# Five blocks of 464 and 448 tokens in place of six of 384 in the first mixing stage, and memory and normaliser loaded pair by pair

## The chip, the cores and the metric

The kernel runs on one core of a Trainium2 chip. The metric is the device time of one execution in microseconds (us), lower is better. The engines of the core are named as the profile names them: PE multiplies, PEld is its loading of weights, DVE, ACT and POOL work on vectors, and SP issues the DMAs.

## The reference

Three computations follow one another on 4 batches of 576 tokens, 2304 in all, with 8 heads of 64 in attention and 512 features after it:

```python
# attention, for each batch and head
a = softmax(causal(q @ k.T / sqrt(64)));  local = a @ v
q_p = where(q > 0, q, exp(q) - 1) + 1
mem = (q_p @ M_prev) / (q_p @ z_prev + 1e-6)
x = g * mem + (1 - g) * local            # g = sigmoid(beta), one number a head
# first mixing stage, 512 -> 2048 -> 512
h = x @ w_in;  y = (h - tanh(h)) @ w_out
# second mixing stage, 512 -> 1024 -> 512
h = y @ w_in2;  s = h * softmax(h)
out = (layernorm(s) * g_ln) @ w_out2
```

The weights of the two mixing stages are float64 in memory; the chip turns them into pairs of float32 numbers.

## The kernel before, in words

**Attention** goes through 16 pairs of heads. Its order is written out by hand in two tables, `PROLOGUE` and `PERIOD`, in which a word such as `load_q:3:-` is one step (name, pair relative to the present one, engine). SP issues every load in that order, so a DMA waits behind the ones before it. `load_batch` brings M_prev (tile `Md`, L110) and z_prev (tile `zb`, L115) for a whole batch of four pairs, at the start of a period. `x_mv` writes the finished pair into `xT` (L420), the transposed tokens.

**The first mixing stage** (`Moe1`) holds all tokens as `xT` and splits each value into a rounded high half `xh` (L573, ACT) and a low half (L575, POOL). The hidden features are cut into 8 slices of 256; for each slice it goes over the token blocks. `h_step` multiplies a block with the slice's `wi`: 2 x 12 multiplications (L589). ACT and DVE then form h - tanh(h) and its two halves (L600 to L603). `y_step` multiplies the result with `wo`: 4 x 6 multiplications (L616), into PSUM tiles `Y` that DVE adds into `yT` (L628 in slice 0, L630 later). Blocks stand one after the other in this order on PE: H of block n+1, Y of block n. A Y tile has two buffers for its first two feature groups and one for the others, so Y of block n+1 waits until DVE has taken Y of block n.

Beside that a `Weights` loader turns the float64 weights of later slices into two float32 halves, a chunk of 128 x 512 at a time: one step on ACT (L732), five on DVE (L734 to L748), a sum on POOL (L750; on DVE in the first blocks), for `w2o` a scaling on POOL (L753), then the high half on ACT (L757) and the low half on POOL (L759; on DVE in the first blocks). `pump` finishes the chunk in work and starts the next; it is called once after each block. Every engine keeps the order of the program.

While the last pairs of attention run, the H multiplications of blocks 0 and 1 of slice 0 stand between them on PE. Behind them come Y of blocks 0 and 1, H of block 2, then the usual order.

**The second mixing stage** (`Moe2`) goes through 18 tiles of 128 tokens: `h_mm` (L796), the maximum (`top`, L807), the norms (`norm`, L816 to L825), transposes (L835) and the output multiplication `o_mm` with the eight blocks of `w2o` (L865). The chunks of `w2o` that the loader has not turned by the end of the first stage are done between `norm(1)` and `top(2)`.

Of the kernel before, what the change touches and what calls it, by code (L numbers as in the profile page):

```python
# [15 lines left out]
P = 128  # L16
# [6 lines left out]
class Attention:  # L23
# [5 lines left out]
    def __init__(self, ap, sp, ps, tc, q, k, v, M_prev, z_prev, beta, xT, ident):  # L29
# [6 lines left out]
        self.read, self.done = 0, 0  # L36
# [380 lines left out]
    def x_mv(self, p):  # L417
        b, h0 = divmod(2 * p, self.H)
        xt, t0 = self.xT(b * self.S)
        self.nc.sync.dma_start(  # L420
            out=xt[:, h0 // 2, t0 : t0 + self.S].bitcast(F32), in_=self.x.pop(p)
        )
# [7 lines left out]
        f_z:0:- load_k:1:- f_red:0:- load_q:2:- k_hd:0:a:0 f_eps:0:- k_ld:0:a:0 s_mm:0:-:4  # L430
# [8 lines left out]
        s_exp:1:-:2 s_norm:0:-:2 s_norm:0:-:1 s_norm:0:-:3 q_lo:2:- load_q:3:- s_mm:2:-:4  # L439
# [8 lines left out]
        load_q:4:- s_mm:3:-:1 s_max:3:-:1 a_t:1:-:3 s_exp:2:-:3 s_max:3:-:2 q_t:3:- q_hi:3:a  # L448
# [19 lines left out]
        s_eps:0:- load_q:3:- q_hi:2:a s_exp:1:-:4 s_mm:1:-:0 s_max:1:-:2 a_pv:-1:-:1  # L468
# [6 lines left out]
    def run(self, filler):  # L475
# [11 lines left out]
        def emit(name, i, engine, part):  # L487
# [40 lines left out]
class Moe1:  # L528
# [5 lines left out]
    NB = 384  # L534

    def __init__(self, tc, w_in, w_out, wpool, tpool, loader):
# [7 lines left out]
        self.w, self.x, self.G = {}, {}, {}  # L544

# [34 lines left out]
    def h_step(self, s, n, H, per=0):  # L580

        nc, KD, KF, NB = self.nc, self.KD, self.KF, self.NB
# [15 lines left out]
        G = self.G[s, n] = self.tp.tile([P, 2, KF, NB], F32R, tag="G", name=f"G{s}_{n}", bufs=2)  # L598
        t = self.tp.tile([P, KF, NB], F32, tag="t", name=f"t{s}_{n}", bufs=1)
# [5 lines left out]
    def y_step(self, s, n, ps, yT):  # L605
        nc, KF, NB = self.nc, self.KF, self.NB
# [5 lines left out]
        for d in range(self.KD):  # L612
# [8 lines left out]
            y = yT[:, d, n * NB : (n + 1) * NB]  # L621
# [3 lines left out]
            if d == 3:  # L625
                y, src = yT[:, 2:4, n * NB : (n + 1) * NB], X[:, :, 0:NB]
# [250 lines left out]
def attention_moe_kernel(  # L877
# [7 lines left out]
    HT = NT // 2  # L885
# [7 lines left out]
    xl = ctx.enter_context(tc.tile_pool(name="xl", bufs=2))  # L893
# [229 lines left out]
```

## Time and profile before

| | us |
|---|---|
| median of 3 runs | 866.45 (865.75 to 867.38) |
| the profiled execution, its own time | 866.64 |
| its span in the trace | 864.8 |
| PE busy | 837.6 (97%) |
| DVE busy | 625.1 (72%) |
| ACT busy | 395.8 (46%) |
| POOL busy | 366.7 (42%) |

The span is what the profiler saw of the execution; 1.84 us of the execution's own time lie around it. A busy share is an average over the whole span, while the stages differ: attention fills the first 250 us, the first mixing stage goes to about 650 us, the second one to the end. A busy time of PE counts multiplications that overlap, so it says less than the start of one block and of the next.

### The profile page before, as it was taken

How to read it: one execution, taken by the hardware profiler on the slowest of the kernel's cores; microseconds unless marked ns; L12 is line 12 of the kernel's file. 1: busy time of each engine (PE TensorE's matmuls, PEld its weight loads, DVE VectorE, ACT ScalarE, POOL GpSimd, SP SyncE). 2: the span in 40 equal slices, each digit the busy share in tenths (PEclk: the TensorE clock that was granted, in tenths of full speed). 3: DMA queues.
4: the chain of work that ended last, by engine and by line, in shares of the span. 5: the costliest groups of instructions: out<-in, count | busy, mean ns of one | idle time of the engine just before them, and what ended most of it. 6: DMA issues, size and time to landing. Idle time of an engine off the chain costs nothing.

```text
span 864.8 us, 13784 instructions
## 1 busy us (share of the span) xinstructions
PE 837.6 (97%) x5016; PEld 752.5 (87%) x5016; DVE 625.1 (72%) x1215; ACT 395.8 (46%) x843; POOL 366.7 (42%) x453
## 2 busy tenths in 40 slices
PE   4999999999999899999999999999999999999998
PEld 3777777777789899999999999999998888888887
DVE  6888889988657877787777877775787655555553
ACT  5898888888744323323233232332322323323222
POOL 6968787887835333333333333430533111111110
PEclk9999999999999999999999999999999999999999
DMA  6896677565110211212112121220200000000001
GB/s 131 198 207 161 161 183 164 146 146 135 45 52 25 74 60 63 74 50 74 54 69 74 49 74 49 74 70 5 72 27 0 25 25 25 20 19 25 25 25 37
DMA packets 82372, 64.66 MB, mean 75 GB/s; under 512 B 63296, under 2 KB 63552, under 8 KB 82304
## 3 DMA queue, kind: packets, MB, share of 16 engines
q1 hardware_dynamic: 82304, 63.78, 27.3%
q8 instruction: 40, 0.66, 0.3%
q14 instruction: 28, 0.23, 0.1%
HBM read 40.90 MB, written 4.72 MB: 53 GB/s over the span
## 4 chain that ended last, share of the span: by engine, by line
PE 73%; DVE 1%; ACT 1%; issue 0%; ACTq 0%
PE Y L616 23%; PE H L589 23%; PE H L796 11%; PE T L835 2%; PE X L400 1%; PE T L381 1%; PE O9X L865 1%; PE O3X L865 1%; PE O13X L865 1%; PE O11X L865 1%; PE O7X L865 1%; PE O5X L865 1%; PE O1X L865 1%; PE O0X L865 1%; PE O15X L865 1%; PE O16S L865 1%
## 5 line engine op out<-in xcount | busy, mean ns | idle before, releaser
L616 PE MATMUL Y<-G,wo 128*128 128x384 f32 x1152 | 209.3, 337 | 3.0 <-DVE yT L628 2.2
L616 PEld LDWEIGHTS Y<-G,wo 128*128 128x128 f32 x1152 | 202.2, 189 | 3.6 <-ACT cva L732 2.5
L589 PE MATMUL H<-xh,wi 128*128 128x384 f32 x768 | 150.7, 337 | 0.0
L589 PEld LDWEIGHTS H<-xh,wi 128*128 128x128 f32 x768 | 134.8, 188 | 1.3 <-issue 0.8
L600 ACT ACTIVATE t<-H 128x768 f32<-128x768 f32 x48 | 39.1, 814 | 197.4 <-PE H L589 193.0
L750 POOL TENSOR_TENSOR cvw<-cvw,cva 128x512 f32<-128x512 f32 x44 | 56.8, 1291 | 164.6 <-DVE cva L748 121.9
L336 POOL TENSOR_SCALAR P<-P,sm,og 128x192 f32<-128x192 f32 (+4 forms) x160 | 105.8, 673 | 23.1 <-DVE sm L331 19.7
L319 ACT ACTIVATE P<-sc,mx 128x192 f32<-128x192 f32 (+4 forms) x160 | 88.8, 558 | 9.1 <-DVE mx L303 8.6
L796 PE MATMUL H<-w2i,Ys 128*128 128x512 f32 x384 | 90.0, 390 | 0.0
L796 PEld LDWEIGHTS H<-w2i,Ys 128*128 128x128 f32 x384 | 72.0, 188 | 15.0
L601 DVE TENSOR_TENSOR t<-H,t 128x768 f32<-128x768 f32 x48 | 45.9, 957 | 51.6 <-ACT t L600 51.6
L381 PEld LDWEIGHTS T<-ident,P 128*128 128x128 f32 x480 | 52.4, 141 | 35.0 <-DVE mx L303 11.1
L589 PE MATMUL H<-xT,wi 128*128 128x384 f32 x384 | 82.8, 337 | 0.0
L303 DVE CUSTOM_DVE_ANT_0 sc<-S,mask 128x64 f32<-128x64 f32 (+4 forms) x160 | 73.1, 486 | 11.5 <-PE S L289 9.1
L381 PE MATMUL T<-ident,P 128*128 128x128 f32 x480 | 73.2, 281 | 7.6 <-DVE mx L303 6.2
L630 DVE TENSOR_TENSOR yT<-Y,yT 128x384 f32<-128x384 f32 (+1 forms) x126 | 79.0, 683 | 0.0
L603 DVE TENSOR_TENSOR G<-t,G 128x768 fp32r<-128x768 f32 x48 | 46.3, 965 | 42.4 <-ACT G L602 42.4
L824 POOL TENSOR_TENSOR s<-s,nhalf 128x1 f32<-128x1 f32 x18 | 9.9, 551 | 153.3 <-DVE s L823 134.5
L602 ACT CAST G<-t 128x768 fp32r<-128x768 f32 x48 | 40.1, 835 | 63.6 <-DVE t L601 63.6
L589 PEld LDWEIGHTS H<-xT,wi 128*128 128x128 f32 x384 | 67.9, 188 | 0.1
L807 DVE TENSOR_REDUCE s<-H 128x1 f32<-128x1024 f32 x18 | 22.0, 1224 | 59.9 <-PE H L796 59.9
L289 PE MATMUL S<-KH,Qs 128*128 128x256 f32 (+3 forms) x192 | 56.2, 330 | 8.2 <-DVE Qs L182 5.3
(285 smaller groups left out, 1427.0 us busy)
## 6 DMA issues: line engine op xcount, KB each, us to landing
raw<-in_moe_w_in_dram SPq DMA_DIRECT2D x24, 512.0 KB, 3.7
raw<-in_moe_w_out_dram SPq DMA_DIRECT2D x24, 512.0 KB, 3.5
xT<-x SPq DMA_DIRECT2D x16, 288.0 KB, 2.4
out_dram<-ob SPq DMA_DIRECT2D x17, 256.0 KB, 2.0
KH<-KH SPq DMA_DIRECT2D x30, 144.0 KB, 2.8
KL<-KL SPq DMA_DIRECT2D x30, 144.0 KB, 2.7
q<-in_q_dram SPq DMA_DIRECT2D x16, 256.0 KB, 3.7
k<-in_k_dram SPq DMA_DIRECT2D x16, 256.0 KB, 3.6
```

Of the source, the lines that this page charges most:

```text
L289: nc.tensor.matmul(t[:, o + a : o + z], lh, K[:, a:z], start=(i == 0), stop=(i == 1), skip_group_check=True,)
L303: self.nc.vector.tensor_tensor_reduce(out=sc, in0=t[:, o : o + W], in1=self.mask[:, self.S - W :], scale=-0.125, scalar=3.0e38, op0=ALU.ad ...
L319: self.nc.scalar.activation(self._p(n, c), self.sc[c], AF.Exp, bias=self.mx[n][:, c : c + 1], scale=-1.0, accum_out=self.sm[n][:, c : c + 1],)
L336: self.nc.gpsimd.tensor_scalar(d, d, self.sm[n][:, c : c + 1], self.og[:, h : h + 1], ALU.mult, ALU.mult)
L381: nc.tensor.transpose(T[:, at : at + P], Pt[:, col : col + P], self.ident)
L589: nc.tensor.matmul(H[:, f], wi[:, wl, c, f * P : (f + 1) * P], self.x[n][xl][:, c], start=(i == 0), stop=(i == 3 * KD - 1),)
L603: nc.vector.tensor_tensor(G[:, 1], t, G[:, 0].bitcast(F32), ALU.subtract)
L616: nc.tensor.matmul(Y[d][:, 0:NB], wo[:, wl, f, d * P : (d + 1) * P], G[:, gl, f], start=(i == 0), stop=(i == 3 * KF - 1),)
L630: nc.vector.tensor_tensor(y, src, y, ALU.add)
L750: self.eng.tensor_tensor(w, w, a, ALU.add)
L796: nc.tensor.matmul(H[:, nh * 512 : (nh + 1) * 512], Y[:, yl, c, :], w2i[:, wl, c, nh * 512 : (nh + 1) * 512], start=(k == 0), stop=(k == 3 ...
L865: nc.tensor.matmul(O, L[:, ll, f, :], self.w2o[f][:, wl, a : a + w], start=(f == 0 and k == 0), stop=(f == KF - 1 and k == 2),)
```

## The change

The token blocks get a list of sizes, 464, 464, 464, 464 and 448, and tiles that were sized by 384 are sized by 464. The two tiles of `xT` hold 928 and 1376 tokens in place of 1152 each; a pair whose tokens cross that border takes two DMAs. `load_batch` becomes `load_mem`, which brings M_prev and z_prev of one pair, three DMAs, and stands in the two tables of attention behind `load_q`; there are three tiles `Md` of one pair each. `pump` is called twice after block 2 of each slice, so that six chunks go with five blocks. One block of `w2o` has a tile of its own in place of two, and three in place of two lie in the room of `xT`.

```diff
-        for i in range(2):
-            t = ap.tile([P, self.HP, P], F32, tag=f"Md{i}", name=f"Md{i}", bufs=1)
+        for i in range(3):
+            t = ap.tile([P, P], F32, tag=f"Md{i}", name=f"Md{i}", bufs=1)
...
-    def load_batch(self, b):
+    def load_mem(self, p):
         nc, D = self.nc, self.D
-        Md = self.Md[b % 2]
+        b, h0 = divmod(2 * p, self.H)
         for j in range(2):
-            nc.sync.dma_start(
-                out=Md[j * D : (j + 1) * D, :, j * D : (j + 1) * D],
-                in_=self.M[b].rearrange("(c j) d e -> j d c e", j=2)[j],
-            )
-        zb = self.zb[b] = self.ap.tile([P, self.HP, 2, D], F32, tag="zb", name=f"zb{b}")
+            a = slice(j * D, (j + 1) * D)
+            nc.sync.dma_start(out=self.Md[p % 3][a, a], in_=self.M[b, h0 + j])
+        z = self.zb[p] = self.ap.tile([P, 2, D], F32, tag="zb", name=f"zb{p}")
         nc.sync.dma_start(
-            out=zb.rearrange("p c j d -> p (c j d)"),
-            in_=self.z[b].rearrange("h d -> (h d)").partition_broadcast(P),
+            out=z.rearrange("p j d -> p (j d)"),
+            in_=self.z[b, h0 : h0 + 2].rearrange("h d -> (h d)").partition_broadcast(P),
         )
...
-        xt, t0 = self.xT(b * self.S)
-        self.nc.sync.dma_start(
-            out=xt[:, h0 // 2, t0 : t0 + self.S].bitcast(F32), in_=self.x.pop(p)
-        )
+        x = self.x.pop(p)
+        for out, a in self.xT(h0 // 2, b * self.S, self.S):
+            self.nc.sync.dma_start(out=out.bitcast(F32), in_=x[:, a : a + out.shape[1]])
...
-        s_eps:0:- load_q:3:- q_hi:2:a s_exp:1:-:4 s_mm:1:-:0 s_max:1:-:2 a_pv:-1:-:1
+        s_eps:0:- load_q:3:- load_mem:2:- q_hi:2:a s_exp:1:-:4 s_mm:1:-:0 s_max:1:-:2 a_pv:-1:-:1
...
-            if batch < self.B and before >= self.HP * (batch - 1):
-                self.load_batch(batch)
-                batch += 1
...
-    NB = 384
+    BLOCKS = (464, 464, 464, 464, 448)
+    NB = max(BLOCKS)
...
-            w2o_part(w2p.tile([P, 2, 2, DM], F32R, tag="w2o", name="w2o"), 2)
+            w2o_part(w2p.tile([P, 2, 1, DM], F32R, tag="w2o", name="w2o"), 1)
...
             else:
                 loader.pump()
+                if n == 2:
+                    loader.pump()
```

Three places show how the instructions move. On DVE, in slice 0 of the first mixing stage, before the change, from the end of the conversion behind block 2 (`cva` and `cvw` are the loader's tiles; `t_3` and `G_3` belong to block 3, `Y_2` to block 2, `wi` is the next slice's weight):

```order
L748 SCALAR_TENSOR_TENSOR cva<-raw,cva 128x512
L750 TENSOR_TENSOR cvw<-cvw,cva 128x512
L601 TENSOR_TENSOR t_3_3873<-H_3_3847,t_3_3873 128x768
L603 TENSOR_TENSOR G_3_3872<-t_3_3873,G_3_3872 128x768
L628 COPY yT<-Y_2_0_3878 128x384
L628 COPY yT<-Y_2_1_3879 128x384
L628 COPY yT<-Y_2_2_3880 128x2x384
L759 TENSOR_TENSOR wi_3723<-cvw,wi_3723 128x512
```

One conversion stands ahead of block 3's activation. The same place with the change:

```order
L739 TENSOR_SCALAR cva<-cvw 128x512
L741 SCALAR_TENSOR_TENSOR cva<-raw,cva 128x512
L743 TENSOR_TENSOR cvw<-cvw,cva 128x512
L752 TENSOR_TENSOR wi_3777<-cvw,wi_3777 128x512
L727 TENSOR_SCALAR cva<-cva 128x512
L730 TENSOR_SCALAR cva<-cva 128x512
L734 SCALAR_TENSOR_TENSOR cvw<-raw,cva 128x512
L739 TENSOR_SCALAR cva<-cvw 128x512
L741 SCALAR_TENSOR_TENSOR cva<-raw,cva 128x512
L743 TENSOR_TENSOR cvw<-cvw,cva 128x512
L593 TENSOR_TENSOR t_3_3940<-H_3_3914,t_3_3940 128x928
L595 TENSOR_TENSOR G_3_3939<-t_3_3940,G_3_3939 128x928
```

A whole second conversion, with the low half of the first ahead of it, now stands ahead of `t_3`, and Y of block 2 behind that as before.

On DVE, at the start of the second mixing stage (`s_1`, `e_1` belong to token tile 1, `s_2` and `H_2` to tile 2), before:

```order
L822 BN_AGGR s_1_7292<-s_1_7292 128x2
L823 TENSOR_SCALAR s_1_7292<-s_1_7292 128x1
L825 TENSOR_SCALAR e_1_7309<-e_1_7309,s_1_7292 128x1024
L807 TENSOR_REDUCE s_2_7350<-H_2_7325 128x1
L817 TENSOR_SCALAR s_2_7350<-s_2_7350 128x1
```

Here the last step of norm(1) is followed by the maximum of tile 2. With the change:

```order
L814 BN_STATS s_1_6837<-e_1_6854 128x6 x2
L815 BN_AGGR s_1_6837<-s_1_6837 128x2
L816 TENSOR_SCALAR s_1_6837<-s_1_6837 128x1
L818 TENSOR_SCALAR e_1_6854<-e_1_6854,s_1_6837 128x1024
L727 TENSOR_SCALAR cva<-cva 128x512
L730 TENSOR_SCALAR cva<-cva 128x512
L734 SCALAR_TENSOR_TENSOR cvw<-raw,cva 128x512
L739 TENSOR_SCALAR cva<-cvw 128x512
L741 SCALAR_TENSOR_TENSOR cva<-raw,cva 128x512
L800 TENSOR_REDUCE s_2_6907<-H_2_6882 128x1
```

The five DVE steps of one more `w2o` chunk stand between the two.

On SP, in the prologue of attention, before (`q`, `KH`, `KL`, `Qs` are the loads and moves of the scores):

```order
L127 DMA q_97<-in_q_dram 128x8x64
L131 DMA q_97<-in_q_dram 64x2x64
L184 DMA KH_1_283<-KH_1_283 64x576
L184 DMA Qs_115<-Qs_113 64x576
L184 DMA KL_1_284<-KL_1_284 64x576
```

The moves come right behind the load of q. With the change:

```order
L125 DMA q_97<-in_q_dram 128x8x64
L129 DMA q_97<-in_q_dram 64x2x64
L111 DMA Md_113<-in_M_prev_dram 64x64 x2
L113 DMA zb_336<-in_z_prev_dram 128x128
L182 DMA KH_1_289<-KH_1_289 64x576
L182 DMA Qs_117<-Qs_115 64x576
L182 DMA KL_1_290<-KL_1_290 64x576
```

Three DMAs for M_prev and z_prev stand ahead of the moves.

## Rows read from the trace of the kernel before

**Rows 1.** The table of stretches (`windows`): from and to in us from the start of the span and the length, then the busy time of PE, PEld, DVE, ACT and POOL with the instructions in brackets, the granted TensorE clock (1.00 is full), the busy share of the DMA engines, and GB/s. The stretches are the steady part of attention, the change from attention to the first mixing stage, the steady part of that stage, and the second mixing stage.

```profile
25.00:200.00 175.00, 168.35 (x1306) 132.00 (x1304) 154.96 (x426) 153.19 (x413) 140.66 (x211) 1.00 0.71 169
...
251.00:292.00 41.00, 38.02 (x209) 37.44 (x209) 30.56 (x39) 16.22 (x30) 19.96 (x18) 0.96 0.09 34
292.00:640.00 348.00, 348.00 (x2002) 348.00 (x2001) 259.60 (x410) 113.94 (x166) 119.52 (x89) 1.00 0.19 61
640.00:865.00 225.00, 221.47 (x1078) 186.23 (x1077) 126.76 (x211) 61.51 (x112) 37.65 (x40) 1.00 0.06 22
```

**Rows 2.** The chain of work that ended last, in order of time: start us, us, and what ran; x24 is one block's 24 multiplications with one kind of weight. L589 and L616 are the two multiplications of the first mixing stage (384 columns each), L796 is the first of the second stage (512 columns). From the row at 297.36 to the row at 643.81 the two kinds of block alternate without a gap, 83 of them, so the first and the last are shown.

```profile
250.64 8.32 PE Y L616 x48
...
297.36 4.18 PE Y L616 x24
...
643.81 5.58 PE H L796 x24
...
683.80 5.45 PE H L796 x24
```

**Rows 3.** The timeline of PE in the change of stages (start us, us, engine, line, operation, tiles, shape, count, and in brackets the idle time before and what ended it): the Y multiplications of blocks 3 and 4 of slice 0.

```profile
276.40 4.40 PE L616 MATMUL Y<-G,wo 128*128 128x384 f32 x24 [0.76 <-ACT xh L573]
...
287.20 6.00 PE L616 MATMUL Y<-G,wo 128*128 128x384 f32 x24 [2.22 <-DVE yT L628]
```

**Rows 4.** The timeline of DVE around the same place, same columns. L759 is the low half of a converted weight chunk, L734 the first and L750 the last of the six DVE operations of a conversion, L601 and L603 the two DVE steps of a block's activation, L628 the copy of Y out of PSUM.

```profile
243.80 0.69 DVE L759 TENSOR_TENSOR wo<-cvw,wo 128x512 fp32r<-128x512 f32 x1 [0.69 <-ACT wo L757]
...
266.75 0.42 DVE L734 TENSOR_SCALAR cva<-cva 128x512 f32<-128x512 f32 x1
...
272.97 0.95 DVE L601 TENSOR_TENSOR t<-H,t 128x768 f32<-128x768 f32 x1
274.83 0.96 DVE L603 TENSOR_TENSOR G<-t,G 128x768 fp32r<-128x768 f32 x1 [0.90 <-ACT G L602]
275.70 1.88 DVE L628 COPY yT<-Y 128x384 f32<-128x384 f32 x3
...
283.17 0.69 DVE L750 TENSOR_TENSOR cvw<-cvw,cva 128x512 f32<-128x512 f32 x1
```

**Rows 5.** The timeline of ACT around the same place: L602 is the rounding of a block's activation, L757 that of a weight chunk.

```profile
265.00 0.84 ACT L602 CAST G<-t 128x768 fp32r<-128x768 f32 x1 [1.02 <-DVE t L601]
...
274.70 0.61 ACT L757 CAST wi<-cvw 128x512 fp32r<-128x512 f32 x1
```

**Rows 6.** The timeline of POOL around the same place: the four low halves of one token block.

```profile
266.89 4.89 POOL L575 TENSOR_TENSOR xT<-xT,xh 128x384 fp32r<-128x384 f32 x4 [4.78 <-ACT xh L573]
```

**Rows 7.** The table of stretches again, for single microseconds after the second wait of rows 3 (columns as in rows 1; the seventh number is the granted clock).

```profile
288.20:289.20 1.00, 1.00 (x5) 1.00 (x4) 0.94 (x3) 0.00 (x0) 0.00 (x0) 0.50 0.00 0
...
291.20:292.20 1.00, 1.00 (x8) 1.00 (x7) 0.81 (x1) 0.16 (x1) 0.91 (x1) 1.00 0.02 4
```

**Rows 8.** The timeline of DVE at the start of the second mixing stage: the first and last DVE operation of a conversion (POOL adds the halves there), the last step of norm(1) (L825) and the maximum of token tile 2 (L807).

```profile
645.06 0.42 DVE L734 TENSOR_SCALAR cva<-cva 128x512 f32<-128x512 f32 x1
...
647.22 0.69 DVE L748 SCALAR_TENSOR_TENSOR cva<-raw,cva 128x512 f32<-128x512 uint32 x1
...
665.92 1.78 DVE L825 TENSOR_SCALAR e<-e,s 128x1024 f32<-128x1024 f32 x1 [0.67 <-POOL s L824]
667.62 1.21 DVE L807 TENSOR_REDUCE s<-H 128x1 f32<-128x1024 f32 x1
```

**Rows 9.** The timeline of POOL in the last blocks of the first mixing stage: one w2o chunk's sum (L750), its scaling (L753) and its low half (L759).

```profile
632.08 1.30 POOL L750 TENSOR_TENSOR cvw<-cvw,cva 128x512 f32<-128x512 f32 x1 [3.48 <-DVE cva L748]
633.47 0.70 POOL L753 TENSOR_SCALAR cvw<-cvw,gl 128x512 f32<-128x512 f32 x1
634.91 1.29 POOL L759 TENSOR_TENSOR w2o_b<-cvw,w2o_b 128x512 fp32r<-128x512 f32 x1 [0.74 <-ACT w2o_b L757]
```

**Rows 10.** The timeline of PE at the start of the second mixing stage: the last six multiplications of the first output tile, which read w2o_c, and the transposes behind them.

```profile
669.51 1.53 PE L865 MATMUL O0X<-w2o_c,L 128*128 128x512 f32 x6
670.88 1.04 PE L835 MATMUL T<-ident,e 128*128 128x128 f32 x8
```

**Rows 11.** The timeline of ACT in the first 20 us: the exponential of the gate table.

```profile
10.15 0.21 ACT L101 ACTIVATE og<-g 128x8 f32<-128x8 f32 x1 [2.12 <-DMA g<-in_beta_dram]
```

**Rows 12.** The timeline of SP, the issues of DMAs, at three places of attention: start us, us that the issue took, line, tiles, count.

```profile
4.30 1.28 SPq L110 DMA_DIRECT2D Md<-in_M_prev_dram  x2
...
6.27 0.43 SPq L96 DMA_DIRECT2D g<-in_beta_dram  x1
...
33.74 0.54 SPq L184 DMA_DIRECT2D KH<-KH  x1
...
113.61 0.74 SPq L131 DMA_DIRECT2D q<-in_q_dram  x1
117.15 0.50 SPq L184 DMA_DIRECT2D Qs<-Qs  x1
```

**Rows 13.** The timeline of PE in the prologue: the first score multiplication of head 4.

```profile
39.59 0.51 PE L289 MATMUL S<-KH,Qs 128*128 128x256 f32 x2
```

**Rows 14.** The page's part 6, DMA issues: out<-in, queue, operation, count, KB each, median us from issue to landing.

```profile
KH<-KH SPq DMA_DIRECT2D x30, 144.0 KB, 2.8
```

**Rows 15.** The chain of work that ended last, where attention ends.

```profile
226.99 1.23 ACT xh L573 x3
...
230.09 1.10 DVE cva L737
```

More of the change, by code (lines that the diff above doesn't have):

```diff
@@ L34, in __init__ @@
         self.between = None
-        self.read, self.done = 0, 0
+        self.done = 0
         self.scores = q.shape[0] * q.shape[1] * (q.shape[2] // P + 1)
@@ L354, in a_mem @@
         nc, S, xo = self.nc, self.S, self.XO
-        b, h0 = divmod(2 * p, self.H)
         self.X = self.ps.tile([P, 1024], F32, tag="X", name=f"X{p}")
-        self.read = p + 1
         for a, z in ((0, 256), (256, S)):
             nc.tensor.matmul(
-                self.X[:, xo + a : xo + z], self.Md[b % 2][:, h0 // 2, :],
+                self.X[:, xo + a : xo + z], self.Md[p % 3],
                 self.fT[p][:, a:z], start=True, stop=False, skip_group_check=True,
@@ L385, in a_ev @@
         T, runs = self.pt[n, gi]
-        pt = self.ap.tile([P, 512], F32, tag="pt", name=f"pt{n}_{gi}", bufs=5)[:, 0 : T.shape[1]]
+        pt = self.ap.tile([P, 448], F32, tag="pt", name=f"pt{n}_{gi}", bufs=5)[:, 0 : T.shape[1]]
         self.copy(pt, T)
@@ L544, in __init__ @@
         self.w, self.x, self.G = {}, {}, {}
+        self.at = [sum(self.BLOCKS[:n]) for n in range(len(self.BLOCKS) + 1)]
     def load_slice(self, s):
@@ L597, in h_step @@
                         yield
-        G = self.G[s, n] = self.tp.tile([P, 2, KF, NB], F32R, tag="G", name=f"G{s}_{n}", bufs=2)
-        t = self.tp.tile([P, KF, NB], F32, tag="t", name=f"t{s}_{n}", bufs=1)
+        G = self.tp.tile([P, 2, KF, self.NB], F32R, tag="G", name=f"G{s}_{n}", bufs=2)
+        G = self.G[s, n] = G[:, :, :, 0:NB]
+        t = self.tp.tile([P, KF, self.NB], F32, tag="t", name=f"t{s}_{n}", bufs=1)[:, :, 0:NB]
         nc.scalar.activation(t, H, AF.Tanh)
@@ L605, in y_step @@
     def y_step(self, s, n, ps, yT):
-        nc, KF, NB = self.nc, self.KF, self.NB
+        nc, KF, NB = self.nc, self.KF, self.BLOCKS[n]
+        t0, t1 = self.at[n : n + 2]
         _, wo = self.w[s]
@@ L902, in attention_moe_kernel @@
     gl = cpool.tile([P, FF2 // P], F32, tag="gl", name="gl")
-    xtiles = [xl.tile([P, KD, HT], F32R, tag="xl", name=f"xT{i}") for i in range(2)]
-    def xT(t0):
-        i, o = divmod(t0, HT)
-        return xtiles[i], o
     loader = Weights(nc, cv)
@@ L912, in attention_moe_kernel, with xT @@
     NB = m.NB
-    nblk = NT // NB
+    nblk = len(m.BLOCKS)
+    assert m.at[nblk] == NT
+    X2 = m.at[2]
+    xtiles = [
+        xl.tile([P, KD, n], F32R, tag=f"xl{i}", name=f"xT{i}") for i, n in enumerate((X2, NT - X2))
+    ]
+    def xT(c, t0, n):
+        a = max(0, min(n, X2 - t0))
+        parts = []
+        if a:
+            parts.append((xtiles[0][:, c, t0 : t0 + a], 0))
+        if a < n:
+            parts.append((xtiles[1][:, c, t0 + a - X2 : t0 + n - X2], a))
+        return parts
     def split_x(n, pool):
-        t, o = xT(n * NB)
-        yield from m.split_x(n, pool, t[:, :, o : o + NB])
+        i = n // 2 and 1
+        o = m.at[n] - i * X2
+        yield from m.split_x(n, pool, xtiles[i][:, :, o : o + m.BLOCKS[n]])
     eb = ExitStack()
@@ L1010, in more_loads @@
         if (s, n) == (m.NS - 1, 2):
-            t = xl.tile([P, KD * HT], F32R, tag="xl", name="w2o_c")
+            t = xl.tile([P, KD * X2], F32R, tag="xl0", name="w2o_c")
             n = KF2 - len(w2o)
```

24 lines of the change are left out of this document (10 added, 14 removed).

## Prediction

> **What bounds the kernel now.** I read the table of stretches first [rows 1]. In the steady first mixing stage (292 to 640 us) PE is busy for the whole stretch, DVE for 75% and the others for a third, and the second stage leaves PE idle for 3.5 of 225 us. In both, only what PE does or waits for counts. In attention PE, DVE, ACT and POOL all lie between 80 and 96%, and each hands to the others, so there a change counts only if it makes somebody late. Between the stages (251 to 292 us) PE loses 3 us and the granted clock falls to 0.96. Then the chain of waits in order of time [rows 2]: it gives PE's pace free of overlaps. 83 groups of 24 multiplications lie between 297.36 and 643.81, so one of 384 columns costs 346.45 / 83 / 24 = 173.9 ns; one of 512 columns costs 5.45 / 24 = 227.1 ns. The slope is 53.2 / 128 = 0.4154 ns a column, and 14.4 ns belong to each multiplication whatever its length. Last, the timelines of the places where the order changes: the change of stages [rows 3 to 7], the start of the second stage [rows 8 to 10], the loads in attention [rows 11 to 15].
>
> **Part 1, fewer multiplications.** 8 slices x 48 x 6 blocks = 2304 become 1920. By the line above 464 columns cost 173.9 + 80 x 0.4154 = 207.1 ns and 448 cost 200.5. Before: 2304 x 173.9 = 400.7 us. After: 384 x (4 x 207.1 + 200.5) = 395.2. That is -5.5 us, all on PE's path. The bounds take the other readings of the same rows: with 5.58 / 24 = 232.5 ns at 512 the slope is 0.458 and nothing is gained (cost in proportion to the columns); with 4.18 / 24 = 174.2 at 384 and 227.1 at 512 it is 401.3 - 395.3, -6.0. I take -5.5, since the 5.45 row is the steady one.
> The Trainium skill, page "TensorE: Matmul & The Clock Gate", section "Back-to-back issue gap", gives an isolated multiplication N / 2.4 + 2.5 ns at full clock: the 384 that go would save 384 x 2.5 ns = 1.0 us by it, an estimate that speaks against the change. Its slope agrees with the rows, its fixed part does not (14 ns), and the measurement decides; by the page the forecast would be 4.5 us higher.
>
> **Part 2, two conversions behind block 2 in the steady stage.** DVE has per block two activation steps, three additions and a conversion; PE's block grows to 9.95 us (48 x 207.1 ns). DVE's own work, scaled by 464 / 384 from rows 4 (0.95, 0.96 and 1.88 us), is 1.15 + 1.16 + 2.27 + 2.85 for the conversion [rows 8] = 7.4 us. With a second conversion it is 10.3, and the second one also waits for sum, rounding and ACT's step, some 2.6 us. So DVE falls behind by about 4 us once a slice and has 2.5 us less the wait between its steps (0.9), some 1.6 us, in each of the four other blocks. The activation of a block is wanted only one block (5 us of PE) later, and that cover holds 4 us. I cost it at 0, with 0 to +5 as bounds; the last slice, whose chunks have a scaling too, is the tightest.
>
> **Part 3, the change of stages.** PE starts Y of block 0 at 250.64 [rows 2]. Eight groups later, without a wait, Y of block 4 would start at 250.64 + 8 x 4.174 = 284.03; it starts at 287.20 [rows 3], so 3.2 us are waits. Behind them the clock stands at 0.50 for some 3 us [rows 7], and the 24 multiplications take 6.00 in place of 4.17: 1.8 us. With the change there are three token blocks left to split in place of four, but two conversions stand ahead of block 3's activation on DVE. From PE's first Y on: Y0 and Y1 to 9.95, H2 to 14.9, H3 to 19.9, Y2 to 24.9, H4 to 29.7, then Y3. DVE's path for Y3: from H2's end tanh 1.0 (ACT and a hand-over), subtraction 1.15, rounding 1.0 [rows 5], low half 1.15: 19.4. Conversion with its sum on DVE 2.85 + 0.69 [rows 8, 4]: 22.95. High half on ACT 0.6 [rows 5], low half on DVE 0.7 [rows 4]: 24.25. The second conversion falls beside POOL's split of block 4 [rows 6], where one took 272.97 - 266.75 = 6.2 us [rows 4]: 30.45. Block 3's subtraction, rounding and low half 1.15 + 1.0 + 1.15: 33.75. The first copy of Y2, which frees the PSUM tile that Y3 wants: 34.4 to 34.5. PE waits 4.8 us instead of 3.2. The next wait (block 4) goes: DVE's copies of Y2 end at 36.0, then low half 0.7, conversion and sum 3.5, block 4's three steps 3.3, Y3's first copy 0.6: 44.1, and PE, after Y3 and the next H, wants its tile at 34.5 + 2 x 4.97 = 44.4. I take +1.6, with the clock's fall as before. Bounds: -5.0 (no wait and no fall) to +3.4 (a second fall).
>
> **Part 4, the extra `w2o` chunk at the start of the second stage.** Five blocks with six calls leave one chunk more than before: seven chunks in the last slice for six calls. It is turned between norm(1) and top(2). The last step of norm(1) ends at 667.62 [rows 8]; conversion 2.85 + hand-over: 670.6; POOL's sum and scaling, from 632.08 to 634.17 [rows 9]: 672.7; ACT's high half, to the start of the low half at 634.91: 673.4; low half 1.29: 674.7. In the old time PE wants the last block of `w2o` three multiplications before 670.88 [rows 10], at 670.2. Two of the three then remain behind 674.7, so it ends at 675.2: +4.3 us, I write +4.4 with the wake-up. Nothing later gives it back, since PE stays the bound; DVE's norm(2) is late by as much. This wait of 3.2 us, then one multiplication, then 1.2 us, is longer than the one of rows 3, behind which the clock fell; I add the same +1.8. Bounds +3.5 to +6.5.
>
> **Part 5, loads in attention.** At the start the gate table is issued behind three DMAs [rows 12], and ACT waits 2.12 us for it [rows 11]. These three carry a quarter as much: -0.8 (0 to -2.1). In the prologue SP has no gap from 20 us on and takes three DMAs more after each of two loads of q, as the order shows. Three such issues took 6.27 - 4.30 = 1.97 us for a batch, three short moves 3 x 0.54 = 1.6 [rows 12]; at 1.7 the move of KH issued at 33.74 comes at 37.1 and lands 2.8 later [rows 14], at 39.9, where PE wants head 4's KH at 39.59 [rows 13]. I take +0.5 (0 to +3.9, the whole delay). In the steady periods SP is idle from 114.35 to 117.15 [rows 12], which takes the three issues: 0. The memory multiplication that the new load waits for precedes that gap. At attention's end three splits on ACT and two DVE steps beside POOL's splits lie on the chain [rows 15], each 0.1 to 0.2 us longer with 464 columns: +0.6 (0 to +1.5).
>
> **The sum.** -5.5 + 0 + 1.6 + 4.4 + 1.8 - 0.8 + 0.5 + 0.6 = +2.6 us. The profiled execution took 866.64 us (span 864.8 and 1.84 around it), which gives 869.2; the median of the runs is 0.2 lower: 869.0.
>
> **Rivals.**
> - The clock holds behind the wait of part 4: -1.8, 867.2. For it: earlier waits of 0.76 us left the clock alone [rows 3]. Against it: this wait is longer than the 2.22 us that did not.
> - The waits between the stages vanish (faster): DVE is the place, the price is -5.0 in place of +1.6, 862.4. For it: one split less, and rows 4 show steps that run at half their length without POOL. It decides at the end of the second conversion: at 25.8 or before instead of 30.45, as 3.9 us of steps follow and PE comes at 29.7. Against it: the order puts it there, and ACT's rounding and the low half lie between the two conversions.
> - SP's queue in the prologue makes attention late by 3.9 us: 872.4. For it: no gap there. Against it: the heads before have their data.
> - DVE overruns in each slice: 0.7 us in seven slices, 873.9. For it: POOL's low half runs beside the second conversion, and rows 4 show what that costs. Against it: some 1 us is left by the count of part 2.
> - No fixed part in a multiplication's cost: 874.5; the 5.45 us of rows 2 speaks against it.
>
> **How the numbers follow.** A measurement of this kernel tells about 0.2%, 1.7 us, from no change. Forecast 0.43 (slower 0.34, same 0.08, faster 0.01, as 868.2 lies 0.8 us below it); clock holds 0.20 (same 0.15, slower 0.02, faster 0.03); waits vanish 0.14 (faster 0.13, same 0.01); SP 0.11 (slower 0.10, same 0.01); overrun 0.09 (slower 0.07, same 0.02); no fixed part 0.03 (slower 0.02, same 0.01). Together slower 0.55, same 0.28, faster 0.17. The range 863.2 to 872.5 holds the forecast, the clock's rival, most of SP's and the upper edge of the vanished waits. The likeliest case alone lies between 867.5 and 870.5.
>
> **What would show it.** In the new profile: 24 multiplications of 464 columns in 4.97 us on the chain; one wait of PE ahead of Y of block 3 in slice 0, none ahead of block 4; about 4.4 us of waiting inside the first output tile, put down to the loader's POOL or ACT step on w2o_c, and a clock of 0.50 behind it; the steady stage without idle PE; head 4's scores not more than 1 us later. The prediction is wrong if the first output tile does not wait, if PE never waits between the stages, or if the steady stage shows DVE as releaser in every slice.

## The result and the profile after

The changed kernel takes **877.72 us** (median of 4 runs, 877.25 to 878.42) against 866.70 for the kernel before beside it: a ratio of **1.0129, 95% interval 1.0111 to 1.0146**. I forecast 869.0 and a range up to 872.5: the sign was right, the size was not. The profiled execution took 877.25 us (span 875.5), so it is compared with the 866.64 us (span 864.8) of before: +10.7 us of span.

Four points of the chain of waits cut that difference into places. In before they are the rows at 250.64 and 643.81 of [rows 2] and at 670.88 of [rows 10]; of after, the fences below show them. A multiplication that follows another without a wait begins 0.17 us earlier in its row of the timeline than in its row of the chain, which is added where only the timeline shows it.

| stretch | before, us | after, us | difference | forecast |
|---|---|---|---|---|
| start to the first Y | 250.6 | 253.6 | +3.0 | +1.9 |
| first Y to the first H of the second stage | 393.2 | 392.5 | -0.65 | -6.1 |
| from there to the second group of transposes | 27.2 | 32.9 | +5.6 | +5.0 |
| from there to the end | 193.8 | 196.5 | +2.7 | +1.8 |

The forecast of the first row is Part 5's +0.3 and 48 multiplications ahead of the first Y that are 33.2 ns longer (1.6); the second is the rest of Part 1 and Part 3; the third is the wait of Part 4 and one last Y of 448 columns (0.6), the fourth the clock of Part 4. So 5.5 of the 8.1 us by which the span was missed lie in the second row.

The table of stretches of after, to be read beside [rows 1] (the change of stages, the steady first stage, the second stage):

```profile
254.00:295.00 41.00, 37.49 (x174) 32.07 (x173) 28.80 (x36) 14.79 (x25) 15.64 (x12) 1.00 0.11 38
295.00:640.00 345.00, 344.56 (x1651) 309.44 (x1649) 251.10 (x361) 109.25 (x149) 117.04 (x84) 1.00 0.19 59
646.00:875.00 229.00, 222.34 (x1057) 184.75 (x1055) 129.03 (x216) 62.58 (x113) 39.48 (x43) 0.99 0.06 24
```

PE is still busy through the whole first mixing stage, with 17% fewer instructions than before: each must be longer by a fifth. The clock between the stages is 1.00 (0.96 before); the second stage now has 6.7 us without PE in place of 3.5.

The chain of work that ended last gives the pace [rows 2]; H L580 and Y L609 are the two multiplications of the first stage now, H L789 and O L858 the two of the second, T L828 the transposes:

```profile
253.63 10.08 PE Y L609 x48
...
328.90 5.07 PE Y L609 x24
333.97 4.89 PE H L580 x24
...
434.20 4.89 PE H L580 x24
...
679.00 1.71 PE T L828 x8
680.71 6.21 PE H L789 x24
...
687.78 5.58 PE O1X L858 x24
```

From 333.97 to 434.20 lie two slices: 50.1 us each. A slice of before is 6 x 2 groups of 346.45 / 83 = 4.174 us [rows 2]: 50.1 us. **The steady stage has gained nothing**: 24 multiplications of 464 columns take 5.00 to 5.08 us, 5.04 on the mean (210 ns each), where I forecast 4.97.

The timeline of PE between the stages [rows 3], where brackets hold the idle time and what ended it:

```profile
281.29 0.47 PE L580 MATMUL H<-xT,wi 128*128 128x448 f32 x1 [0.17 <-POOL xT L566]
282.57 0.47 PE L580 MATMUL H<-xT,wi 128*128 128x448 f32 x1 [0.80 <-POOL xT L566]
284.10 0.47 PE L580 MATMUL H<-xT,wi 128*128 128x448 f32 x1 [1.06 <-POOL xT L566]
...
288.49 5.27 PE L609 MATMUL Y<-G,wo 128*128 128x464 f32 x24 [1.48 <-DVE yT L621]
```

The same view at the end of the last slice and at the start of the second stage [rows 10]:

```profile
640.83 5.31 PE L609 MATMUL Y<-G,wo 128*128 128x464 f32 x24 [1.27 <-DVE yT L623]
645.98 0.40 PE L789 MATMUL H<-w2i,y 128*128 128x512 f32 x1
```
```profile
676.42 0.79 PE L858 MATMUL O0X<-w2o_c,L 128*128 128x512 f32 x1 [3.28 <-ACT w2o_c L750]
677.78 1.22 PE L858 MATMUL O0X<-w2o_c,L 128*128 128x512 f32 x2 [0.56 <-POOL w2o_c L752]
```

And the stretch behind the last two of these waits [rows 7]; the seventh number is the granted clock:

```profile
676.00:680.00 4.00, 3.02 (x9) 2.21 (x10) 1.86 (x4) 2.70 (x6) 2.51 (x2) 0.50 0.00 0
```

Three short waits on POOL's split of x and one of 1.48 us leave the clock at 1.00 (the row of 254 to 295 us above); behind the 3.28 us it stands at 0.50, the lower level, as it did behind the 2.22 us of before.

### The profile page after: what moved, and what is told of

Its sections match the earlier page's. It is cut to its first block, busy times and chain, and to the rows that moved or that the text cites. A ratio compares the mean times of both kernels' runs of the same rounds, so it can differ in the third digit from the quotient of the medians.

```text
span 875.5 us, 13016 instructions
## 1 busy us (share of the span) xinstructions
PE 842.0 (96%) x4632; PEld 712.8 (81%) x4632; DVE 623.1 (71%) x1177; ACT 393.1 (45%) x823; POOL 364.6 (42%) x448
## 4 chain that ended last, share of the span: by engine, by line
PE 65%; DVE 7%; ACT 2%; POOL 1%; issue 1%; DVEq 0%; ACTq 0%; POOLq 0%
PE H L580 21%; PE Y L609 20%; PE H L789 9%; PE T L828 2%; PE X L395 1%; PE T L376 1%; DVE yT L623 1%; DVE cvw L734 1%; DVE cva L741 1%; DVE G L595 1%; PE O12X L858 1%; PE O10X L858 1%; PE O7X L858 1%; PE O5X L858 1%; PE O2X L858 1%; PE O16S L858 1%
## 5 line engine op out<-in xcount | busy, mean ns | idle before, releaser
L609 PE MATMUL Y<-G,wo 128*128 128x464 f32 (+1 forms) x960 | 207.1, 371 | 2.8 <-DVE yT L621 1.5
L609 PEld LDWEIGHTS Y<-G,wo 128*128 128x128 f32 x960 | 180.0, 188 | 23.9 <-ACT cva L725 3.4
L580 PE MATMUL H<-xh,wi 128*128 128x464 f32 (+1 forms) x640 | 148.4, 372 | 0.0
L580 PEld LDWEIGHTS H<-xh,wi 128*128 128x128 f32 x640 | 119.5, 188 | 14.9 <-issue 1.3
L743 POOL TENSOR_TENSOR cvw<-cvw,cva 128x512 f32<-128x512 f32 x43 | 55.6, 1292 | 173.5 <-DVE cva L741 173.5
L592 ACT ACTIVATE t<-H 128x928 f32<-128x928 f32 (+1 forms) x40 | 37.5, 938 | 124.8 <-PE H L580 124.6
L789 PE MATMUL H<-w2i,Ys 128*128 128x512 f32 x384 | 90.8, 392 | 0.0
L789 PEld LDWEIGHTS H<-w2i,Ys 128*128 128x128 f32 x384 | 72.6, 190 | 15.2
L580 PE MATMUL H<-xT,wi 128*128 128x464 f32 (+1 forms) x320 | 80.9, 373 | 2.0 <-POOL xT L566 2.0
L594 ACT CAST G<-t 128x928 fp32r<-128x928 f32 (+1 forms) x40 | 38.6, 964 | 93.5 <-DVE t L593 93.5
L623 DVE TENSOR_TENSOR yT<-Y,yT 128x464 f32<-128x464 f32 (+3 forms) x105 | 77.0, 789 | 0.0
L595 DVE TENSOR_TENSOR G<-t,G 128x928 fp32r<-128x928 f32 (+1 forms) x40 | 44.9, 1122 | 40.2 <-ACT G L594 40.2
L593 DVE TENSOR_TENSOR t<-H,t 128x928 f32<-128x928 f32 (+1 forms) x40 | 44.6, 1114 | 39.8 <-ACT t L592 39.8
L580 PEld LDWEIGHTS H<-xT,wi 128*128 128x128 f32 x320 | 59.8, 188 | 9.3 <-POOL xT L566 3.0
```

The lines of the kernel that those rows point to most:

```text
L580: nc.tensor.matmul(H[:, f], wi[:, wl, c, f * P : (f + 1) * P], self.x[n][xl][:, c], start=(i == 0), stop=(i == 3 * KD - 1),)
L595: nc.vector.tensor_tensor(G[:, 1], t, G[:, 0].bitcast(F32), ALU.subtract)
L609: nc.tensor.matmul(Y[d][:, 0:NB], wo[:, wl, f, d * P : (d + 1) * P], G[:, gl, f], start=(i == 0), stop=(i == 3 * KF - 1),)
L623: nc.vector.tensor_tensor(y, src, y, ALU.add)
L743: self.eng.tensor_tensor(w, w, a, ALU.add)
L789: nc.tensor.matmul(H[:, nh * 512 : (nh + 1) * 512], Y[:, yl, c, :], w2i[:, wl, c, nh * 512 : (nh + 1) * 512], start=(k == 0), stop=(k == 3 ...
```

## The experiments

Theory: blocks of 464 and 448 gain nothing per column, and the chunk of `w2o` that comes late, the waits at both ends of the stage and the longer blocks ahead of the first Y are what is left. Rivals: the moved loads of attention, or how the tiles lie in memory. Each time stands beside runs of the kernel before on the same chip, whose medians differ (865.9 in experiments 1 to 3, 866.4 in 6 and 7, 867.2 in 8 and 9, 865.5 in 10); from one of these groups to another the ratios are the safer comparison.

**1. Six blocks again, with the new loads.** This undoes the blocks and leaves the pair-by-pair loads.

```
-    BLOCKS = (464, 464, 464, 464, 448)
+    BLOCKS = (384,) * 6
...
-                if n == 2:
-                    loader.pump()
...
```

> The changed kernel with six blocks of 384 again, one call of the loader after each block and two blocks of w2o in their own tile: what is left of the change is the loads pair by pair and the other cut of xT. If the blocks and the calls of the loader are the whole cost: 866.7 us like the kernel before, first Y of the first mixing stage at 250.6. If the loads cost what the first Y's start in the new trace leaves after the longer blocks (2.99 - 48 x 0.0364 = 1.2 us): 867.9, first Y at 251.9. A slice takes 50.1 us either way.

Measured: 867.19 us, ratio 1.0001 (0.9986 to 1.0016). The loads and the other cut of `xT` cost nothing that the time shows, and its interval is 1.3 us either way; the loss belongs to the blocks and their calls. In the profiled execution the first Y starts at 251.3 us, between the two values expected and 0.7 us later than before, so a cost below 1 us stays open.

**2. No chunk left for the second stage.** The call that was made only half behind the last block of slice 6 is made as everywhere else, so that all chunks are turned by the time the second stage starts.

```
-            if i < 2 or (s, n) == (m.NS - 2, nblk - 1):
+            if i < 2:
```

> The changed kernel, with the loader also called after the last block of the last slice but one, so that no w2o chunk is left for the second mixing stage. If the late chunk holds up the first output tile by 3.84 us and the half clock behind it costs another 1.6: 872.2 us, no wait of PE in the first output tile, clock 1.00 there. If the wait only moves: 877. If the wait goes and the clock falls all the same: 873.8.

Measured: 871.35 us, ratio 1.0053 (1.0036 to 1.0069): -6.4 us. The chain shows the first output tile without a wait:

```profile
668.92 5.58 PE O0X L858 x24
674.50 0.87 PE T L828 x8
```

Part 4 is shown, wait and clock together: forecast 6.2 us, measured 6.4 (the medians of the two kernels; 6.6 by their ratios).

**3. The second call of slice 0 later**, behind block 4 in place of block 2.

```
-                if n == 2:
+                if n == (2 if s else 4):
```

> The changed kernel, with the second call of the loader in slice 0 after block 4 in place of block 2, so that one conversion stands ahead of block 3's activation as before the change. If the order of DVE makes the waits between the stages (4.8 us of idle PE from 281 to 288.5 us, H of block 4 and Y of block 3): about 874.5 us, H of block 4 without more than 0.8 us of wait. If the splitting of block 4 on POOL makes them: 877.

Measured: 876.68 us, ratio 1.0111 (1.0083 to 1.0139): 1.0 us less than the kernel after by the medians, and the two intervals overlap. The waits on POOL and DVE are gone, so the second call made them; the weights of slice 1 are late in their place, and from 294 to 296 us, behind these waits, the clock stands at 0.50. From the first Y to the second stage the kernel takes 392.6 us, as the kernel after does (392.5):

```profile
292.02 1.11 PE L580 MATMUL H<-xh,wi 128*128 128x464 f32 x4 [2.31 <-ACT wi L750]
293.76 1.14 PE L580 MATMUL H<-xh,wi 128*128 128x464 f32 x2 [0.63 <-POOL wi L752]
```

With five blocks in slice 0 a chunk has one block less in which to be finished, so a later call only moves the loss; the call must go earlier (below).

**4. The pace by itself.** 144 multiplications for each number of columns, operands ready, DVE copying the last result of each. The distance between two copies is the time of 144.

> Multiplications alone, 144 of each size in one stream, same number format, weights reloaded for each; nothing of the reference is computed. Theory 'in proportion' (what the new trace suggests): 0.453 ns a column, so 116 ns at 256 columns, 174 at 384, 203 at 448, 210 at 464, 232 at 512. Theory 'fixed part' (the prediction's): 14 ns beside 0.4154 ns a column, so 121, 174, 200.5, 207 and 227. Theory 'layout': 464 columns cost about 3 ns less when rows start at multiples of 512 columns (b464) than when they are packed (a464).

The timeline of DVE: the row of a size ends its stream. "b" keeps slices 512 columns apart, "a" as many as it multiplies.

```profile
46.47 0.69 DVE L53 COPY o<-a 128x512 f32<-128x512 f32 x1 [46.47 <-PE a L49]
71.45 0.56 DVE L53 COPY o<-a 128x384 f32<-128x384 f32 x1 [24.29 <-PE a L49]
101.77 0.64 DVE L53 COPY o<-a 128x464 f32<-128x464 f32 x1 [29.76 <-PE a L49]
131.53 0.62 DVE L53 COPY o<-a 128x448 f32<-128x448 f32 x1 [29.11 <-PE a L49]
161.76 0.64 DVE L53 COPY o<-b 128x464 f32<-128x464 f32 x1 [29.61 <-PE b L49]
...
307.71 0.59 DVE L53 COPY o<-a 128x416 f32<-128x416 f32 x1 [26.38 <-PE a L49]
328.83 0.49 DVE L53 COPY o<-a 128x320 f32<-128x320 f32 x1 [20.53 <-PE a L49]
346.11 0.42 DVE L53 COPY o<-a 128x256 f32<-128x256 f32 x1 [16.79 <-PE a L49]
378.77 0.69 DVE L53 COPY o<-e 128x512 f32<-128x512 f32 x1 [32.24 <-PE e L49]
```

Divided by 144: 173.5 ns at 384 columns, 120.0 at 256, 226.8 at 512. The slope is 53.3 / 128 = 0.416 ns a column from 384 to 512 and 0.418 from 256 to 384: **the line of rows 2, with its fixed part, is real at these sizes. 464 does not lie on it**: 210.6 ns ("a") and 209.9 ("b"), 3 to 4 ns above it, which is 0.454 a column, the same as the 0.452 of 384. 448 took 206.7, 6 to 7 ns above it.

**5. Where the operands lie.** The same with other offsets and distances, since the output multiplications of the second stage, unchanged by the change, took 5.58 us for 24 in the kernel after (its second output tile, at 687.78, like the ones behind it) and 5.48 to 5.54 before, 228 to 231 ns each. (The 226 to 227 in the expectation is the second stage's H, which takes 5.45 us in both kernels.)

> Leaves out the whole computation: streams of 144 multiplications each, all operands ready, differing in columns, in the distance between the moving slices, in their offset and in the offset of the stationary slice. The first such kernel showed 226.8 ns at 512 columns, 173.5 at 384, 146.7 at 320 and 120.0 at 256, which lie on one line with a fixed part of 14 ns, but 210.2 at 464 and 206.7 at 448, 3 and 6 ns above that line. Theory 'the number of columns itself': 448 and 464 keep their excess (206 to 207 and 209 to 211 ns) whatever the distance and the offset, and 512 and 384 keep 226.8 and 173.5 at every offset. Theory 'where the operand lies': 448 at a distance of 512 falls to 200 to 201, and 512 at an offset of 16 or 32 columns rises to 230 or more. The multiplications of the second stage took 230 to 233 ns in the kernel with five blocks and 226 to 227 in the one with six, at 512 columns both; only the second theory, or an offset of the stationary operand, could explain that.

The timeline of DVE again: "wu" is 512 columns without an offset, "ma", "mb", "mc" move the moving operand by 16, 32, 64 columns of 4 bytes, "sa", "sb" and "sc" the stationary one ("md" ends the stream ahead of "sa"); "fa", "fc" and "fd" are 448 columns, "ga" and "gb" 464.

```profile
81.16 0.69 DVE L56 COPY o<-wu 128x512 f32<-128x512 f32 x1 [31.95 <-PE wu L52]
114.14 0.69 DVE L56 COPY o<-ma 128x512 f32<-128x512 f32 x1 [32.29 <-PE ma L52]
147.61 0.69 DVE L56 COPY o<-mb 128x512 f32<-128x512 f32 x1 [32.78 <-PE mb L52]
180.27 0.69 DVE L56 COPY o<-mc 128x512 f32<-128x512 f32 x1 [31.97 <-PE mc L52]
212.91 0.69 DVE L56 COPY o<-md 128x512 f32<-128x512 f32 x1 [31.95 <-PE md L52]
246.51 0.69 DVE L56 COPY o<-sa 128x512 f32<-128x512 f32 x1 [32.91 <-PE sa L52]
279.98 0.69 DVE L56 COPY o<-sb 128x512 f32<-128x512 f32 x1 [32.78 <-PE sb L52]
312.67 0.69 DVE L56 COPY o<-sc 128x512 f32<-128x512 f32 x1 [32.00 <-PE sc L52]
341.86 0.62 DVE L56 COPY o<-fa 128x448 f32<-128x448 f32 x1 [28.49 <-PE fa L52]
...
400.41 0.62 DVE L56 COPY o<-fc 128x448 f32<-128x448 f32 x1 [28.74 <-PE fc L52]
429.44 0.62 DVE L56 COPY o<-fd 128x448 f32<-128x448 f32 x1 [28.41 <-PE fd L52]
459.84 0.64 DVE L56 COPY o<-ga 128x464 f32<-128x464 f32 x1 [29.77 <-PE ga L52]
489.92 0.64 DVE L56 COPY o<-gb 128x464 f32<-128x464 f32 x1 [29.43 <-PE gb L52]
```

512 columns take 229.0, 232.4 and 226.8 ns with the moving operand off by 64, 128 and 256 bytes, and 233.3, 232.4 and 227.0 with the stationary one off by as much. So **at 512 columns an offset of 64 or 128 bytes costs 2 to 7 ns, and one of 256 bytes nothing**. Each stream moves one operand only, so whether the distance between the two counts, as I take it from here on, or the place of each by itself, these streams do not tell. At 384 it cost 0 (64 bytes) and 2.4 ns (128). 464 columns took 211.1 and 208.9 with offsets of 128 and 256 bytes: there most of the excess is the size. 448 fell to 201.6 to 204.0 at all four layouts tried, lowest at a distance of 464 columns ("fd"), which is no multiple of 256 bytes; so the layout theory is not shown for it, and the 206.7 of experiment 4 stays unexplained.

**6. Five blocks of sizes that lie on the line**: 384, 384, 512, 512, 512, on top of experiment 2. To make room, `cvw` goes, and `xh` of blocks 0 and 1 is as wide as these.

```
-    BLOCKS = (464, 464, 464, 464, 448)
+    BLOCKS = (384, 384, 512, 512, 512)
...
-            w = self.pool.tile([P, N], F32, tag="cvw", name="cvw", bufs=1)
+            w = top.bitcast(F32)
```

> The kernel after with blocks of 384, 384, 512, 512 and 512, the chunk for the second stage done a slice earlier as in no_late_chunk, and, to make room, the first two halves of x kept at 384 columns and the converted weights written over the raw ones. Theory 'a fixed part at 384 and 512 that 464 and 448 lose again': a slice takes 48 x (2 x 173.9 + 3 x 227.1) ns = 49.4 us in place of 50.1, about -5.3 us in all; the first Y starts where it did before (blocks of 384 ahead of it), -3 against no_late_chunk; so 862 to 864 us against the 871.4 of no_late_chunk, and a ratio to the kernel before of 0.995 to 0.998. Theory 'cost in proportion to columns': slices stay at 50.1 us, 867 to 869 us. In both the waits between the stages may shift by 2 us either way.

Measured: 867.85 us, ratio 1.0014 (1.0003 to 1.0025), 3.5 us less than experiment 2, but 4 us over what was expected, and inside the range of the rival: the time alone does not decide between the two. A slice takes 49.9 us, less than the rival's 50.1 and more than the 49.4 expected. Between the stages PE now waits on POOL's split of x with the clock at or near 0.50 behind it (from 284 to 288 us):

```profile
281.37 0.50 PE L580 MATMUL H<-xT,wi 128*128 128x512 f32 x1 [0.92 <-POOL xT L566]
283.04 0.50 PE L580 MATMUL H<-xT,wi 128*128 128x512 f32 x1 [1.17 <-POOL xT L566]
```

The chain of the next experiment, with the same blocks, shows the other part.

**7. The same, with slice 0's second call earlier**, behind block 1.

```
-            if i < 2:
+            if i < 1:
...
-                if n == 2:
+                if n == 2 and s:
```

> As blocks_384_512, with the second pump of slice 0 (behind block 2) moved to block 1. Theory 'the two conversions of block 2 delay the split of x of block 4 and the copies of Y': the waits between 275 and 300 us shrink by 1 to 3 us, and the time by as much. Rival 'the conversions only move to where the first Y's copies stand': the same time within 1 us, with the waits earlier; if the weights of slice 1 come late, as in second_call_later, 1 to 2 us slower.

Measured: 864.34 us, ratio 0.998 (0.997 to 0.999): -3.5 us. The waits on POOL's split of x and the clock's fall are gone, and one wait of 1.5 us on DVE is left: from the first Y to the second stage the profiled execution is 2.9 us shorter. Its first Y is 1.6 us earlier too (251.2 against 252.8 us), which the moved call does not touch: in the profiled execution of experiment 6 PE waits 1.64 us in attention's prologue ahead of head 4's scores (at 41.28 us), and the clock is at 0.50 from 42 to 45 us. The chain shows two kinds of groups of 512 columns:

```profile
393.18 5.49 PE Y L609 x24
...
427.80 5.55 PE H L580 x24
433.34 5.60 PE Y L609 x24
...
443.13 5.60 PE Y L609 x24
```

5.60 / 24 = 233.3 ns: what experiment 5 shows for an offset. From 393.18 to 443.13 lies one slice, 49.95 us. The halves of x for blocks 2 to 4 and every second slice's weights are allocated from the far end of the memory, and by the sizes of the tiles lie 32 bytes off the others modulo 256 (no trace shows an address).

**8. A tile of 32 bytes in front.**

```
     gl = cpool.tile([P, FF2 // P], F32, tag="gl", name="gl")
+    pad = cpool.tile([P, 8], F32, tag="pad", name="pad")
+    nc.gpsimd.memset(pad, 0.0)
```

> blocks_384_512_early with one more tile of 32 bytes a partition ahead of the others, which moves x, its halves, G and every second slice's weights by 32 bytes; now they lie a whole number of 256 bytes from the halves of x and the weights of the other slices, which stand at the far end of the memory. Theory 'distance between the stationary and the moving operand': the multiplications of 512 columns took 230.5 to 232.7 ns on the mean in blocks_384_512_early (227 in some slices, 231 to 236 in the others) and should now take 227 nearly everywhere: 144 of them a slice x 3.5 ns = 0.5 us a slice, 3.5 to 4 us in all, so 860 to 861 us; a slice 49.4 us in place of 49.95. Rival 'the 512 columns cost that beside the other engines': no change, 864 to 865 us.

Measured: 862.25 us, ratio **0.9945 (0.9931 to 0.9959)**, and the same groups of the chain:

```profile
389.67 4.18 PE H L580 x24
...
428.27 5.44 PE H L580 x24
433.71 5.44 PE Y L609 x24
439.15 4.18 PE H L580 x24
```

A slice (389.67 to 439.15) takes 49.5 us in place of 49.95 and of 50.1 before. The medians of experiments 7 and 8 differ by 2.1 us, their ratios by 3.0, of the forecast 3.5 to 4. From the first Y to the second stage the profiled execution is 2.9 us shorter (385.9 in place of 388.8): two waits on DVE that are 0.7 us longer together take back a part of the eight slices' gain. In the profiled execution attention hides a part of this: the clock falls in its prologue as in experiment 6, behind a wait of 1.62 us, and the first Y comes at 252.8 in place of 251.2 us.

**9. Blocks of 464 with everything but the pace mended**: experiment 2, the earlier call of experiment 7, and 128 bytes ahead of the second stage's transposed tiles, which in the kernel after lie 128 bytes off `w2o` by the sizes of the tiles.

```
+            if i == 0:
+                pad = m2.tp.tile([P, 32], F32, tag="pad", name="pad", bufs=1)
+                nc.gpsimd.memset(pad, 0.0)
...
```

> no_late_chunk (blocks of 464 and 448) with two changes that the trace tells apart: the second pump of slice 0 moved from block 2 to block 1, and a tile of 128 bytes a partition ahead of the transposed tiles of the second stage, so that these lie a whole number of 256 bytes from w2o. Theory: the waits on POOL xT and DVE yT between 281 and 291 us (2.0 and 1.5 us in no_late_chunk) shrink to 1.5 us or less, -2 to -3.5 us; a token tile of the second stage takes 11.83 us in place of 11.91, -1.3 us; together 866.5 to 868 us against 871.4. What stays over the kernel before is then the longer blocks ahead of the first Y (2 to 3 us) less what the stages' change gives back. Rival: the token tile stays at 11.91 us (the five-block kernels' w2o in other pieces is the cause), 868 to 869 us.

Measured: 865.83 us, ratio 0.9986 (0.9974 to 0.9997), below what any theory gave. PE's only wait between the stages is short, and a token tile of the second stage is the distance between the next two rows:

```profile
284.81 5.27 PE L609 MATMUL Y<-G,wo 128*128 128x464 f32 x24 [0.98 <-DVE yT L621]
```
```profile
699.82 1.03 PE L828 MATMUL T<-ident,e 128*128 128x128 f32 x8
711.59 1.03 PE L828 MATMUL T<-ident,e 128*128 128x128 f32 x8
```

11.77 us, against 11.91 in experiment 2 (on the mean of 14 tiles 11.78 and 11.91; before 11.83):

```profile
704.53 1.04 PE L828 MATMUL T<-ident,e 128*128 128x128 f32 x8
716.44 1.03 PE L828 MATMUL T<-ident,e 128*128 128x128 f32 x8
```

16 token tiles make 2.2 us; the stretch from the first Y to the second stage is 3.8 us shorter than in experiment 2 (388.7 in place of 392.5), where 2 to 3.5 were forecast. So five blocks of 464 need not be slower than six of 384; their pace alone is worth nothing either way.

**10. The best of both**: experiment 8 with the tile of row statistics at 128 bytes, so that the second stage's operands lie multiples of 256 bytes apart too.

```
-        s = self.st[i]["s"] = self.tp.tile([P, 16], F32, tag="s", name=f"s2_{i}")
+        s = self.st[i]["s"] = self.tp.tile([P, 32], F32, tag="s", name=f"s2_{i}")
...
```

> blocks_384_512_pad with the small tile of row statistics of the second stage at 128 bytes a partition in place of 64 (two buffers of it), so that the operands of the second stage, too, all lie whole numbers of 256 bytes apart; in blocks_384_512_pad the first chunk of w2o and the transposed tiles lay 128 bytes off one another. Theory of the distance: a token tile of the second stage takes 11.78 us as in tail_early_pad, in place of 11.84: -0.06 x 16 = -1.0 us, 861 to 861.5 us against 862.25, the first stage unchanged at 49.5 us a slice. Rival: 11.84 us stays, 862 to 862.5 us.

Measured: 861.12 us, ratio **0.9947 (0.9933 to 0.9960)**, the fastest kernel of the study, though not told apart from experiment 8 (0.9945). Two transposes of its steady second stage stand at 707.95 and 719.73, 11.78 us apart, as forecast.

## Why the prediction was wrong

**Part 1 failed: -5.5 us came to nothing (+0.2: eight slices of 50.1 us each, as before).** The step was the line through 384 and 512 columns, read at 464 and 448. Its ends are right (experiment 4, and 5.44 us for 24 at 512 columns in experiment 8), but 464 takes 209 to 211 ns and not 207.1, in the kernel and alone. 4 x 464 + 448 columns then cost what six times 384 cost: 50.1 us a slice. The bound "cost in proportion to the columns" stood in Part 1, and the rival "no fixed part" (874.5, 0.03) foretold this effect with another reason; I dismissed it because two sizes had a fixed part, and no row showed the size in question.

**Part 2**: as forecast in the steady slices, where no slice waits for DVE. The last slice, which I named as the tightest, is not hidden: PE waits 1.27 us, at 640.83. From 293.76 to the first H of the second stage lie 56 groups of 464 columns (5.04 us) and 14 of 448 (4.88), 350.8 us, which took 352.4: 1.6 us were lost, where I had put 0.

**Part 3**: forecast +1.6 us, measured 0.0. From the first Y to the end of Y of block 3 (253.63 to 293.76) lie seven groups, 35.2 us at their pace, so 5.0 us are lost; before, ten groups of 4.174 us lie between 250.64 and 297.36, and 5.0 are lost too, 1.8 of them to the clock. So I had the loss of 4.8 us by waiting nearly right, by luck: it stands at two places, not one. The brackets show 3.5 us of waits (3.0 before), 2.0 of them where the multiplications of block 4 wait for POOL's split of x, which I had counted only as what slows DVE; and a wait costs more than its bracket, since a multiplication that stands alone between two takes 0.47 us and not 0.20. Experiments 3 and 9 show that the waits on POOL hang on the second call. The clock, which I had expected to fall behind them, stays at 1.00.

**Part 4 was right**: 3.28 + 0.56 us of waits inside the first output tile (4.4 forecast), put down to the loader's ACT and POOL steps on `w2o_c`, and a clock of 0.50 behind them. Taking the chunk away gave back 6.4 us (forecast 6.2). The rival "clock holds" falls.

**Part 5**: forecast +0.3 us, and the first Y comes 3.0 us later, of which the 48 longer multiplications ahead of it take 1.7 and 1.3 are left. Experiment 1 has the new loads and shows no loss in its time, so SP's rival of 872.4 falls. But head 4's scores come at 40.77 us after and 40.83 in experiment 1 (39.59 before), later than the 1 us that I allowed, and in the profiled executions of experiments 6 and 8 the wait ahead of them ends in a fall of the clock. The first Y of the kernels with two blocks of 384 ahead of it lies between 250.6 and 252.8 us, so one execution can't tell what the loads are worth within 1 us or so.

**What the sum lacked.** The second stage's token tiles took 0.07 us more each on the mean, 1.2 us, though their instructions were not changed. Experiment 9 took this back and 0.8 us more by moving their operands 128 bytes; that the new sizes had moved them is argued from the sizes of the tiles. With the measured terms the sum is 0.2 + 1.6 + 0.0 + 6.4 + 1.3 + 1.2 = 10.7 us, the 10.7 by which the span grew.

## What to carry to other kernels

Before a tile is resized for fewer instructions, measure the very size: two sizes on a line do not vouch for one between them, and here three blocks of 512 and two of 384 were worth 1.2% of a slice over six of 384 while 464 were worth nothing. A change of tile sizes moves every later tile's address: where a stage that was not touched changes its pace, look at the offset of its two operands. And count a call schedule at its ends (first slice, last slice, first tile of the next stage), since the steady part hid all of it here, and the ends cost 6.4 us in one place.

## What the runs showed of the hardware that I had not expected

- The time of a multiplication is not one line in its columns: 120.0, 146.7, 173.5 and 226.8 ns at 256, 320, 384 and 512, but 209 to 211 at 464 and 202 to 207 at 448. The streams of experiment 4 also had 416, 480 and 496 columns: 187.8, 216.7 and 225.7 ns, which is 1, 3 and 6 ns above the line, so 496 columns cost nearly what 512 do. Why they lie above it stays open.
- At 512 columns an offset of 64 or 128 bytes in the stationary or the moving operand cost 2 to 7 ns of 227, one of 256 bytes nothing (experiment 5); a tile of 32 bytes gave 0.5 us of 49.95 a slice in experiment 8.
- The clock stood at 1.00 through waits of 0.80, 1.06 and 1.48 us after, and through a single one of 1.91 in experiment 8 (at 284.82 us). It fell to 0.50 behind one of 3.28, one of 2.22 (before), one of 1.64 in the prologue of experiment 6, behind 2.31 and 0.63 us in experiment 3, and behind 0.92 and 1.17 us with one multiplication between them (experiment 6). The length of the last wait alone does not tell.
